# Forming twelve segments' value projections while a two-layer kernel's weights load, and reordering the loads

## The chip, the cores and the metric

The kernel runs on one core of one Trainium2 chip. A core has a tensor engine (PE, with weight loads shown apart as PEld), a vector engine (DVE), a scalar engine (ACT), GpSimd (POOL), and SyncE (SP), which here does nothing but issue DMAs. The metric is the device time of one execution in microseconds (us); the figure for a kernel is the median over its runs. The profile is that of a single execution.

## What is computed

Two kinds of layers alternate: A, B, A, B. Each adds to a residual stream x of 2048 tokens of width 512, after a layer norm. Layer A is a recurrent attention with a memory of 8 rows; layer B is a dense layer with a relu. Both A layers share their weights, and so do both B layers.

```python
# A: S = 2048, Dm = 512, H = 32 heads, Dh = 128, M = 8 memory rows, seg_len = 32
mem = mem0
for s in range(n_seg):                      # 64 segments, one after the other
    xs = x[:, s * seg_len:(s + 1) * seg_len, :]
    h = concat([mem, xs])                   # 40 rows
    q, k, v = h @ Wq, h @ Wk, h @ Wv        # 32 heads of 128
    p = softmax(where(mask, q @ k.T * scale, -1e9))
    o = (p @ v) @ Wo
    mem = o[:, :M, :]                       # handed to the next segment
    outs.append(o[:, M:, :])
# B: h = relu(x @ w1) @ w2, inner width 1376
x = x + A(layernorm(x)); x = x + B(layernorm(x))
x = x + A(layernorm(x)); x = x + B(layernorm(x))
```

The memory rows chain the segments of a layer one behind the other. The token rows of a segment do not depend on the chain: in the first layer their layer norm, and so their values `v`, can be formed at any time once x and Wv are there.

## The kernel before

**Tiling over time.** `step(k)` works on segment k of the first attention layer (index 0) and at once on segment k - 4 of the second (index 1), for k from 0 to 67 (`DELTA` is 4). `act` lists the layers that take part; in steps 0 to 3 it is only layer 0, in the last four only layer 1. Blocks of 64 tokens (two segments) pass through output projection, dense layer and residual in filler work that lies between the pieces of the steps; the dense layer first runs in step 3.

**A step.** HT holds the 40 transposed input rows of each layer: 8 memory columns (copied from the PSUM tile `mt` of the step before by DVE, L671) and 32 token columns (L535, or L391 and on for the second layer). Heads go in two halves of 16. For each half: `qk` forms Q and K (L404), then `scores` (L438), `exponents`, `probabilities`, `transpose_p` (L476) and `weighted_v` (L491, tile `pv`). Scores of the second half follow only after the first half's probabilities have been transposed. At the end `output_mem` (L445) multiplies the memory rows with Wo, ACT copies the result to `wm_sb` (L653), four matmuls turn it into `mt` (L668), and DVE and ACT copy that into the next step's HT and HTm (the memory rows alone).

**Values.** `weighted_v` reads the values from one tile Vs, rows 0 to 39 for layer 0 and 64 to 103 for layer 1, tokens in the rows from M = 8 on. `group_values` (L240) forms values for up to 32 rows at a time, four matmuls side by side in 32-column strips of the array, 512 output columns each; a segment takes two groups of 16. ACT copies each group to a tile VmS (L245, three buffers), and a DMA puts it into DRAM (L246); later `load` (L275) brings rows into Vs. The memory rows' values go that way in each step (tile `vmd`), the token rows' through `vd`.

In the first layer, segments 0 to 3 and all odd segments have their token values formed by `values0`: segment 0 in step 0, 1 and 2 in steps 0 and 1 between scores and the second half, and from segment 3 on segment k + 3 at the end of the even step k, after `mt`. Even segments from 4 on ride in free columns of the memory rows' group (`rider`, `first_rider`) and cost no matmuls.

**Order.** The main part lies in a block in which the program order is the order on PE, DVE, ACT and SP. POOL is not among them; its instructions are placed by the scheduler, as are the loads before the block. SP issues nearly all DMAs from one queue, in order; step 0 uses POOL's queue for its values. Tiles in PSUM: three buffers `c`, two `fill`, one for each layer's scores, one for the output projection.

**Loads.** The weights come in 1 MB pieces (8 heads of one matrix): Wq and Wk pieces 0 and 1, four of Wv, Wq and Wk pieces 2 and 3, four of Wo. The token rows come as pairs of 128 rows (`load_pair`), normalized and transposed by `pair_moments`, `pair_normalize` and `pair_T`. `load_dense` loads w1 and w2 in step 1.

Of the kernel before, what the change touches and what calls it, by code (L numbers as in the profile page):

```python
# [7 lines left out]
BF = mybir.dt.bfloat16  # L8
F32 = mybir.dt.float32
# [13 lines left out]
def kernel(  # L23
# [14 lines left out]
    nc = tc.nc  # L38
    _, S, Dm = A_x.shape
# [5 lines left out]
    L = M + SEG  # L45
# [33 lines left out]
    def load_pair(n):  # L79
        pairs["x", n] = wk.tile([128, Dm], BF, tag="xe", bufs=1, name="xe")  # L80
        nc.sync.dma_start(out=pairs["x", n][:], in_=A_x[0, 128 * n:128 * n + 128, :])
# [22 lines left out]
    Wo_v = A_Wo.rearrange("h e d -> e h d")  # L104
    PW = H * Dh // 4
    hh = H // 4

    def load_w(W_sb, W_v, pc):
        nc.sync.dma_start(out=W_sb[:, :, pc * PW:(pc + 1) * PW], in_=W_v[:, :, pc * PW:(pc + 1) * PW])  # L109

    for pc in range(2):
        load_w(Wq_sb, Wq_v, pc)
        load_w(Wk_sb, Wk_v, pc)
    for pc in range(4):
        load_w(Wv_sb, Wv_v, pc)
    for pc in range(2, 4):
        load_w(Wq_sb, Wq_v, pc)
        load_w(Wk_sb, Wk_v, pc)
    for pc in range(4):
# [4 lines left out]
    def load_dense():  # L124
        nc.sync.dma_start(out=w1_sb[:], in_=B_w1.rearrange("(c p) f -> p c f", p=128))
        nc.sync.dma_start(out=w2_sb[:, 0:NFC - 1, :],
                          in_=B_w2[0:(NFC - 1) * 128, :].rearrange("(c p) d -> p c d", p=128))
        nc.sync.dma_start(out=w2_sb[0:F_LAST, NFC - 1, :], in_=B_w2[(NFC - 1) * 128:Dff, :])
# [37 lines left out]
    nc.gpsimd.memset(P[:], 0.0)  # L166
    PT = const.tile([128, 8, 2, L], BF)
    OTx0 = const.tile([128, 2, H // 2, 128], BF)
    nc.vector.memset(OTx0[:], 0.0)
    OTx1 = const.tile([128, H // 2, 128], BF)  # L170
    nc.vector.memset(OTx1[:], 0.0)
    OTm = const.tile([128, H, 32], BF)
    nc.gpsimd.memset(OTm[:], 0.0)
    wm_sb = const.tile([128, Dm], BF)
    xn1 = const.tile([128, Dm], BF)
    nc.gpsimd.memset(xn1[:], 0.0)

# [23 lines left out]
        nc.vector.tensor_scalar(out=out[sl, :], in0=R[sl, :], scalar1=mv[sl, 0:1], scalar2=rstd[sl, 0:1],  # L201
                                op0=ALU.subtract, op1=ALU.mult)

    def transpose_x(xn, tag, bufs):
        tp = ps_fill.tile([128, NC4, 128], BF, tag="fill")
        for c4 in range(NC4):
            nc.tensor.transpose(tp[:, c4, :], xn[:, c4 * 128:(c4 + 1) * 128], ident[:])  # L207
        xnT = wk.tile([128, NC4, 128], BF, tag=tag, bufs=bufs, name=tag)
        nc.scalar.copy(out=xnT[:], in_=tp[:])
        return xnT  # L210


# [8 lines left out]
    def pair_T(n):  # L221
        pairs["T", n] = transpose_x(pairs["n", n], "xnT0", 2)

    def tokens_T(s, lo, n):

        c = SEG * (s % 4) + lo
        return pairs["T", s // 4][:, :, c:c + n]

# [2 lines left out]
    def group_values(lhsT, ii, dst, pool, tag, q, lo=0, hi=NC4):  # L233
        if lo == 0:
            vps[tag] = pool.tile([128, 512], F32, tag=tag, name="vp")
        vp = vps[tag]
        for c4 in range(lo, hi):
            for j in range(4):
                n = 4 * ii + j
                nc.tensor.matmul(vp[32 * j:32 * j + 32, :], lhsT=lhsT(c4), rhs=Wv_sb[:, c4, n * 512:(n + 1) * 512],  # L240
                                 start=(c4 == 0), stop=(c4 == NC4 - 1), tile_position=(0, 32 * j))
        if hi < NC4:
            return
        VmS = wk.tile([128, 512], BF, tag="VmS", bufs=3, name="VmS")
        nc.scalar.copy(out=VmS[:], in_=vp[:])  # L245
        q.dma_start(out=dst[ii].rearrange("j t e -> (j t) e"), in_=VmS[:])  # L246

    def dram_values(name, tag, bufs):
        return dram.tile([2, 4, 32, 512], BF, tag=tag, bufs=bufs, name=name)
# [5 lines left out]
    def values0(s, ii, q=None, lo=0, hi=NC4):  # L255

        if ii == 0 and lo == 0:
            vds[0, s] = dram_values("vd0", "vd0", 4)
        t = tokens_T(s, 0, SEG)
        group_values(lambda c4: t[:, c4, :], ii, vds[0, s], *((ps_fill, "fill") if ii else (ps_c, "c")), q or nc.sync, lo, hi)  # L260
# [14 lines left out]
        q.dma_start(out=Vs[lo:lo + n, 2048 * ii:2048 * (ii + 1)].rearrange("t (j e) -> t j e", j=4),  # L275
                    in_=vd[ii, :, t:t + n, :].rearrange("j t e -> t j e"))

    def load_tokens0(k, q):
        for ii in range(2):
            if first_rider(k):  # L280
                load(q, ii, M, 16, vmds[k - 2], 16)
                load(q, ii, M + 16, 16, vmds[k - 1], 16)
            else:
                load(q, ii, M, SEG, vds[0, k], 0)
# [173 lines left out]
            nc.scalar.activation(out=es[:], in_=es[:], func=ACTF.Exp, scale=SCALE)  # L458
        return ess

    def probabilities(hf, ess, a):

        es = ess[a]
        sm = wk.tile([128, 8], F32, tag="sm", bufs=2, name="sm")
        nc.vector.tensor_reduce(out=sm[:], in_=es[:], axis=AX.X, op=ALU.add)  # L465
        nc.vector.reciprocal(out=sm[:], in_=sm[:])
        eng = nc.vector if hf == 1 and a == max(ess) else nc.gpsimd
        eng.tensor_tensor(out=P[:, :, 64 * a:64 * a + L], in0=es[:],  # L468
                          in1=sm[:].unsqueeze(2).to_broadcast([128, 8, L]), op=ALU.mult)

# [40 lines left out]
    def step(k):  # L511
# [17 lines left out]
        with tc.high_priority(offset=PRIO):  # L529
            for a in act:  # L530
                if k == a * DELTA:
                    nc.vector.tensor_copy(out=HT[:, :, a, 0:M], in_=mem0T[:])
                    nc.vector.tensor_copy(out=HTm[:, :, a * M:(a + 1) * M], in_=mem0T[:])
            if 0 in act:
                nc.gpsimd.tensor_copy(out=HT[:, :, 0, M:L], in_=tokens_T(k, 0, SEG))  # L535
        if pr is not None:
            pair_moments(pr)

# [8 lines left out]
        qks = qk(HT, 0, act, after0)  # L547
        if dw is not None:
            dense_T(dw)
        if k == 0:  # L550
            for ii in range(2):
                values0(0, ii, nc.gpsimd)
        q = nc.gpsimd if k == 0 else nc.sync
        with tc.high_priority(offset=PRIO):
            if 0 in act:
                load_tokens0(k, q)
            vmds[k] = dram_values("vmd", "vmd", 4)
            for ii in range(2):
                group_values(lambda c4: HTm[:, c4, :], ii, vmds[k], ps_c, "c", q)
            if 1 in act and even:  # L560
                values1(k, 0)
            for ii in range(2):
                for a in act:
                    load(q, ii, 64 * a, M, vmds[k], a * M)
                if 1 in act and (ii == 0 or not even):
                    load(q, ii, 64 + M, SEG, vds[1, k], 0)
            scores(qks, act)
            if 1 in act and even:
                values1(k, 1)
                load(q, 1, 64 + M, SEG, vds[1, k], 0)  # L570
# [3 lines left out]
            ess = exponents(act)  # L574
        if dw is not None:
            dense_h(dw, 2, 3)
        if k < 2:
            for ii in range(2):
                values0(k + 1, ii)
        if k == 1:  # L580
            load_dense()
        if ldp is not None:
            load_pair(ldp)
        if not even and p + 1 < NP and p >= 1:
            load_x(p + 1)

        def after1(n):
            if n == 0:
                probabilities(0, ess, act[-1])
            if n == 1:  # L590
                masks(act, 1)

        if len(act) > 1:
            probabilities(0, ess, act[0])
        qks = qk(HT, 1, act, after1)

        def v0(ii):
            if even and k + 3 < NSEG:
                values0(k + 3, ii)

        def v1(ii):
            if even and k >= DELTA:
                values1(k + 1, ii)
# [10 lines left out]
            ess = exponents(act)  # L614


        v1(0)
        if dw is not None:
            dense_y(dw, 0, NFC)
# [6 lines left out]
            output_x(nw, 0, XA)  # L626
        with tc.high_priority(offset=PRIO):
            for a in act:
                probabilities(1, ess, a)
            if first:  # L630
                hand_on(dw)
            transpose_p()
            if first:
                block_moments(dw + 2)
        if dw is not None and dw >= 2:
            store(dw)
        if w is not None:
            output_x(w, XE, H)
        if nw is not None:
# [40 lines left out]
    with tc.manual_schedule(engines={mybir.EngineType.PE, mybir.EngineType.DVE, mybir.EngineType.SP,  # L680
                                    mybir.EngineType.Activation}):
        mem0T = const.tile([128, NC4, M], BF)
        tp = ps_fill.tile([128, NC4, 128], BF, tag="fill", name="tp0")
        for c4 in range(NC4):
            nc.tensor.transpose(tp[:, c4, :], mem0[:, c4 * 128:(c4 + 1) * 128], ident[:])
        nc.vector.tensor_copy(out=mem0T[:], in_=tp[:, :, 0:M])
        pair_moments(0)
        pair_normalize(0)
        pair_T(0)
        load_pair(1)  # L690
        for k in range(NSTEP):
            step(k)
        i = NT - 1
        output_x(i, XD, H)
        add_output(i)
        dense_moments(i)
        dense_normalize(i)
        dense_T(i)
        dense_h(i, 0, 3)
        dense_y(i, 0, NFC)  # L700
        store(i)
# [35 lines left out]
```

## Time and profile before

| what | us |
|---|---|
| median of 3 runs | 1709.79 (1708.37 to 1710.15) |
| the profiled execution | 1710.79 |
| its span, first to last instruction | 1709.0 |
| PE busy in the span | 1646.5 |
| mean granted clock of PE | 0.989 |

A row of the timeline has the start, the length, the engine, the line of the kernel, the operation, output tile and inputs, partitions by elements, a count where like instructions were merged, and in brackets how long the engine had been idle before it and what ended that. A row of the windows has a stretch of the span, the busy time of PE, of PE's weight loads, of DVE, ACT and POOL with their instruction counts, PE's granted clock, the busy share of the 16 DMA engines and the GB/s they moved. Matmuls are pipelined, so a busy PE isn't always a PE at its peak. A row by tile has the least, median and greatest duration in ns of one instruction, first and last start, and the shape.

### The profile page before, as it was taken

The numbers are of one execution on the slowest core, as the hardware profiler recorded it, in microseconds if no ns is written. First come the engines' busy times: TensorE is split into PE (matmuls) and PEld (weight loads), VectorE is DVE, ScalarE is ACT, GpSimd is POOL, SyncE is SP. The second block draws the span as 40 slices with busy tenths as digits, with TensorE's granted clock in tenths as the row PEclk, the third lists the DMA queues.
The fourth block names the chain that finished last, engine by engine and source line by source line (L and its number), as shares of the span: only waits on it lengthen the run. The fifth ranks groups of instructions, "written<-read, shape, count | busy, mean of one in ns | idle before, by whom it ended". The sixth has DMA issues, their size and how long they took to land.

```text
span 1709.0 us, 84178 instructions
## 1 busy us (share of the span) xinstructions
PE 1646.5 (96%) x37785; PEld 1202.4 (70%) x37876; DVE 1062.8 (62%) x2534; ACT 870.1 (51%) x2413; POOL 244.4 (14%) x457
## 2 busy tenths in 40 slices
PE   4799999999999999999999999999999999999997
PEld 2577777776777777677777767777776777777766
DVE  2356666666766666676666667666666766666644
ACT  1345555555555555555555555555555555555543
POOL 3011111111111111111111111111111111111100
PEclk9799999999999999999999999999999999999999
DMA  9612122121212212121221212122121212112111
GB/s 349 190 41 70 58 66 61 54 67 54 69 59 65 62 53 67 53 69 59 66 60 54 66 54 67 61 66 60 55 66 54 69 58 68 54 54 63 42 45 35
DMA packets 115513, 118.90 MB, mean 70 GB/s; under 512 B 14040, under 2 KB 106240, under 8 KB 115152
## 3 DMA queue, kind: packets, MB, share of 16 engines
q1 hardware_dynamic: 112240, 108.46, 20.4%
q8 instruction: 297, 4.87, 1.3%
q0 software_dynamic: 2912, 5.05, 1.1%
q14 instruction: 64, 0.52, 0.1%
HBM read 65.74 MB, written 45.61 MB: 65 GB/s over the span
## 4 chain that ended last, share of the span: by engine, by line
PE 93%; SPq 2%; DMA 2%; issue 1%; DVE 1%; ACT 0%; POOL 0%; POOLq 0%; DVEq 0%; ACTq 0%
PE qp L404 35%; PE vp L240 18%; PE wox L305 12%; PE sp L445 7%; PE hp L340 5%; PE pv L491 4%; PE yp L359 4%; PE sp L438 4%; PE tp L476 3%; SPq L109 2%; DMA Wo_sb<-in_A_Wo_dram 1%; SPq L120 1%; PE tp L207 1%; PE wox L289 1%; DMA vd<-VmS 1%
## 5 line engine op out<-in xcount | busy, mean ns | idle before, releaser
L404 PE MATMUL qp<-HT,Wq_sb 128*128 128x80 bf16 (+1 forms) x8704 | 370.0, 200 | 5.0 <-ACT VmS L245 3.1
L404 PE MATMUL qp<-HT,Wk_sb 128*128 128x80 bf16 (+1 forms) x8704 | 369.6, 200 | 2.8 <-DMA Wk_sb<-in_A_Wk_dram 2.8
L410 DVE CAST KT<-qp 128x480 bf16<-128x480 f32 (+3 forms) x340 | 202.8, 597 | 264.4 <-PE qp L404 259.0
L404 PEld LDWEIGHTS <-Wq_sb 128*128 128x128 bf16 x8704 | 330.1, 100 | 41.2 <-issue 33.7
L404 PEld LDWEIGHTS <-Wk_sb 128*128 128x128 bf16 x8704 | 328.7, 100 | 3.1 <-DMA Wk_sb<-in_A_Wk_dram 3.1
L408 ACT CAST QT<-qp 128x480 bf16<-128x480 f32 (+3 forms) x340 | 173.1, 509 | 254.3 <-PE qp L404 254.2
L245 ACT CAST VmS<-vp 128x512 bf16<-128x512 f32 x332 | 194.0, 585 | 162.3 <-PE vp L240 153.0
L305 PE MATMUL wox<-Wo_sb,OTx 128*128 128x512 bf16 x899 | 223.9, 379 | 9.9 <-issue 9.7
L468 POOL TENSOR_TENSOR P<-es,sm 128x320 bf16<-128x320 f32 x188 | 136.0, 723 | 580.2 <-ACT QT L408 155.9
L453 DVE TENSOR_REDUCE mx<-sp 128x8 f32<-128x320 f32 x256 | 114.5, 487 | 150.0 <-PE sp L438 149.6
L465 DVE TENSOR_REDUCE sm<-es 128x8 f32<-128x320 f32 x256 | 120.6, 471 | 73.2 <-ACT es L458 65.2
L305 PEld LDWEIGHTS <-OTx 128*128 128x128 bf16 x960 | 83.0, 98 | 104.5 <-issue 26.9
L240 PE MATMUL vp<-Wv_sb,HT 128*32 128x512 bf16 x2048 | 134.2, 382 | 0.0
L445 PE MATMUL sp<-Wo_sb,OTm 128*32 128x512 bf16 x2144 | 131.2, 387 | 1.4 <-DMA Wo_sb<-in_A_Wo_dram 1.4
L240 PE MATMUL vp<-Wv_sb,HTm 128*32 128x512 bf16 x2176 | 131.1, 382 | 0.0
L507 DVE CAST OTx<-pv 128x256 bf16<-128x256 f32 x256 | 91.2, 418 | 36.9 <-ACT OTm L499 35.9
L458 ACT ACTIVATE es<-es 128x320 f32<-128x320 f32 x256 | 109.3, 467 | 9.3 <-DVE es L456 2.8
L456 DVE TENSOR_TENSOR es<-sp,mx 128x320 f32<-128x320 f32 x256 | 113.4, 482 | 0.6
L477 ACT CAST PT<-tp 128x320 bf16<-128x320 f32 x136 | 58.3, 428 | 90.6 <-PE tp L476 90.6
L499 ACT CAST OTm<-pv 128x64 bf16<-128x64 f32 x512 | 80.4, 225 | 45.1 <-PE pv L491 45.0
L507 ACT CAST OTx<-pv 128x256 bf16<-128x256 f32 x256 | 84.8, 385 | 32.5 <-PE pv L491 32.5
L196 POOL TENSOR_TENSOR rstd<-rstd,mhalf_t 128x1 f32<-128x1 f32 (+1 forms) x82 | 45.3, 553 | 384.0 <-DVE rstd L195 384.0
(88 smaller groups left out, 1811.4 us busy)
## 6 DMA issues: line engine op xcount, KB each, us to landing
vd<-VmS SPq DMA_DIRECT2D x194, 128.0 KB
Vs<-vd SPq DMA_DIRECT2D x194, 128.0 KB
vmd<-VmS SPq DMA_DIRECT2D x134, 128.0 KB
Vs<-vmd SPq DMA_DIRECT2D x254, 32.0 KB
Vs<-vmd SPq DMA_DIRECT2D x120, 64.0 KB
Wq_sb<-in_A_Wq_dram SPq DMA_DIRECT2D x4, 1024.0 KB
Wk_sb<-in_A_Wk_dram SPq DMA_DIRECT2D x4, 1024.0 KB
R<-in_A_x_dram POOLq DMA_DIRECT2D x32, 128.0 KB, 2.9
```

What stands on the lines that cost most here:

```text
L240: nc.tensor.matmul(vp[32 * j:32 * j + 32, :], lhsT=lhsT(c4), rhs=Wv_sb[:, c4, n * 512:(n + 1) * 512], start=(c4 == 0), stop=(c4 == NC4 - 1 ...
L245: nc.scalar.copy(out=VmS[:], in_=vp[:])
L305: nc.tensor.matmul(wo_tiles[i][:], lhsT=ot, rhs=Wo_sb[:, h, :], start=(h == 0), stop=(h == H - 1))
L404: nc.tensor.matmul(qp[:, hi, 0:ncol], lhsT=W_sb[:, c4, h * Dh:(h + 1) * Dh], rhs=HT[:, c4, a_lo:a_hi, :], start=(c4 == 0), stop=(c4 == NC4 ...
L408: nc.scalar.copy(out=dst[:, 0:nh, a_lo * L:a_hi * L], in_=qp[:, 0:nh, 0:ncol])
L410: nc.vector.tensor_copy(out=dst[:, 0:nh, a_lo * L:a_hi * L], in_=qp[:, 0:nh, 0:ncol])
L445: nc.tensor.matmul(wo[32 * j:32 * j + 32, :], lhsT=OTm[:, h, :], rhs=Wo_sb[:, h, :], start=(h < 4), stop=(h >= H - 4), tile_position=(0, 3 ...
L453: nc.vector.tensor_reduce(out=mxs[a][:], in_=sp_tiles[a], axis=AX.X, op=ALU.max)
L456: nc.vector.tensor_tensor(out=es[:], in0=sp_tiles[a], in1=mxs[a][:].unsqueeze(2).to_broadcast([128, 8, L]), op=ALU.subtract)
L465: nc.vector.tensor_reduce(out=sm[:], in_=es[:], axis=AX.X, op=ALU.add)
L468: eng.tensor_tensor(out=P[:, :, 64 * a:64 * a + L], in0=es[:], in1=sm[:].unsqueeze(2).to_broadcast([128, 8, L]), op=ALU.mult)
L507: copy(out=ot[:, 8 * q:8 * q + 8, c:c + SEG], in_=pvs[q, a][:, :, M:L])
```

## The change

- Loads: Wv's four pieces come first, then Wq and Wk piece by piece in turn, then Wo. The rows of two sets of four odd segments (`SETS[1]`: 5, 7, 9, 11; `SETS[2]`: 13, 15, 17, 19) are loaded in between, by four DMAs a set, into tiles of 128 rows that serve other ends later.
- `set_values(j, lo, hi)` forms values of four segments at once: 128 token rows are the stationary operand, 512 columns of Wv stream, four matmuls make one chunk of 512 columns, eight chunks a set. Chunks are copied by DVE and ACT in turn (set 2: by ACT alone) into `stage(j, n)`, space in w1_sb and w2_sb, and for part of set 2 in OTx0, which are not yet in use. `set_store` then puts a set into DRAM, 1 MB.
- Before step 0: set 0 (segments 0 to 3), the memory rows' values of step 0 and their loads on POOL's queue, set 1, and two chunks of set 2. In step 0: four chunks of set 2 before the second half's probabilities and two before its `weighted_v`.
- `load_tokens0` takes segment 0 straight from `stage`, and the other eleven from the set in DRAM by one DMA of 32 rows. `values0` is gone for these twelve; the others stay as they are.
- SP: sets 0 and 1 are stored in step 0, set 2 in step 1 just ahead of `load_dense`, which now overwrites what the stores read. `load_pair` of step 1 goes ahead of `load_dense`.
- Smaller edits: OTx0 and OTx1 are no longer cleared; steps 0 and 1 copy tokens into HT on DVE, and step 0 multiplies P on DVE, each on POOL before.

```diff
+    SETS = ((0, 1, 2, 3), (5, 7, 9, 11), (13, 15, 17, 19))
+    set_of = {s: (j, n) for j, ss in enumerate(SETS) for n, s in enumerate(ss)}
+    def load_odd(j):
+        odd_x[j] = wk.tile([128, Dm], BF, tag="ob", bufs=1, name="xo") if j == 1 else wm_sb
+        for n, s in enumerate(SETS[j]):
+            nc.sync.dma_start(out=odd_x[j][SEG * n:SEG * n + SEG, :], in_=A_x[0, SEG * s:SEG * s + SEG, :])
...
-    for pc in range(2):
-        load_w(Wq_sb, Wq_v, pc)
-        load_w(Wk_sb, Wk_v, pc)
+    load_w(Wv_sb, Wv_v, 0)
+    load_w(Wv_sb, Wv_v, 1)
+    load_odd(1)
+    load_w(Wv_sb, Wv_v, 2)
+    load_w(Wv_sb, Wv_v, 3)
+    load_odd(2)
     for pc in range(4):
-        load_w(Wv_sb, Wv_v, pc)
-    for pc in range(2, 4):
         load_w(Wq_sb, Wq_v, pc)
         load_w(Wk_sb, Wk_v, pc)
...
+    def set_values(j, lo, hi):
+        xnT = odd_T[j] if j else pairs["T", 0]
+        for n in range(lo, hi):
+            vp = ps_fill.tile([128, 512], F32, tag="fill", name="vp")
+            for c4 in range(NC4):
+                nc.tensor.matmul(vp[:], lhsT=xnT[:, c4, :], rhs=Wv_sb[:, c4, n * 512:(n + 1) * 512],
+                                 start=(c4 == 0), stop=(c4 == NC4 - 1))
+            (nc.scalar.copy if n % 2 or j == 2 else nc.vector.tensor_copy)(out=stage(j, n), in_=vp[:])
+
+    def set_store(j, q):
+        set_dram[j] = dram.tile([128, H * Dh], BF, tag=f"set{j}", bufs=1, name="vset")
+        for lo, hi in ((0, 8),) if j < 2 else ((0, 2), (2, 5), (5, 8)):
...
+            q.dma_start(out=set_dram[j][:, 512 * lo:512 * hi], in_=src)
...
+        if k in set_of:
+            j, n = set_of[k]
+            q.dma_start(out=Vs[M:L, :], in_=set_dram[j][SEG * n:SEG * n + SEG, :])
+            return
...
-        eng = nc.vector if hf == 1 and a == max(ess) else nc.gpsimd
+        eng = nc.vector if k == 0 or hf == 1 and a == max(ess) else nc.gpsimd
...
-                nc.gpsimd.tensor_copy(out=HT[:, :, 0, M:L], in_=tokens_T(k, 0, SEG))
+                (nc.vector if k < 2 else nc.gpsimd).tensor_copy(out=HT[:, :, 0, M:L], in_=tokens_T(k, 0, SEG))
...
-        if k < 2:
-            for ii in range(2):
-                values0(k + 1, ii)
-        if k == 1:
-            load_dense()
         if ldp is not None:
             load_pair(ldp)
+        if k == 0:
+            set_store(0, nc.sync)
+            set_store(1, nc.sync)
+        if k == 1:
+            set_store(2, nc.sync)
+            load_dense()
...
-            if even and k + 3 < NSEG:
+            if even and k + 3 < NSEG and k + 3 not in set_of:
                 values0(k + 3, ii)
...
+        if k == 0:
+            set_values(2, 2, 6)
         v1(0)
...
+        if k == 0:
+            set_values(2, 6, 8)
         if w is not None:
             output_x(w, XE, H)
...
         pair_T(0)
+        odd_moments(1)
+        odd_normalize(1)
+        set_values(0, 0, 8)
+        nc.vector.tensor_copy(out=HTms[0][:, :, 0:M], in_=mem0T[:])
+        memory_values(0, nc.gpsimd)
+        load_tokens0(0)
+        for ii in range(2):
+            load(nc.gpsimd, ii, 0, M, vmds[0], 0)
+        odd_transpose(1)
+        odd_moments(2)
+        odd_normalize(2)
+        set_values(1, 0, 8)
+        odd_transpose(2)
         load_pair(1)
+        set_values(2, 0, 2)
```

## What I predict

> **What bounds the kernel now.** I read the engine totals first, then the span in a few long windows, then the timeline of the start, then the ends of single steps.
>
> ```profile
> PE 1646.5 (96%) x37785; PEld 1202.4 (70%) x37876; DVE 1062.8 (62%) x2534; ACT 870.1 (51%) x2413; POOL 244.4 (14%) x457
> ...
> 0.00:60.00 60.00, 30.20 (x506) 17.92 (x510) 14.52 (x39) 11.96 (x28) 14.61 (x38) 0.83 0.94 310
> 60.00:110.00 50.00, 46.51 (x1238) 34.67 (x1230) 22.96 (x60) 22.85 (x61) 3.96 (x10) 0.94 0.36 112
> 110.00:1609.00 1499.00, 1481.51 (x33922) 1084.59 (x34005) 976.66 (x2317) 795.27 (x2209) 219.67 (x399) 1.00 0.20 60
> ```
>
> After the totals, each row is a window: busy time of PE, PE's weight loads, DVE, ACT and POOL with counts, granted clock, DMA share, GB/s. From 110 us on PE is busy 1481.5 of 1499.0 us: PE work taken out there comes off the time, unless a wait appears in its place. In the first 60 us PE is busy for half and the DMA engines for 0.94: there the weights bound the kernel. So PE work that moves from the second stretch into idle time of the first is worth nearly all of itself.
>
> ```profile
> 20.87 0.61 PE L240 MATMUL vp<-Wv_sb,xnT 128*32 128x512 bf16 x2 [2.17 <-DMA Wv_sb<-in_A_Wv_dram]
> 23.58 1.89 PE L240 MATMUL vp<-Wv_sb,xnT 128*32 128x512 bf16 x14 [2.10 <-DMA Wv_sb<-in_A_Wv_dram]
> ...
> 41.63 0.71 PE L404 MATMUL qp<-HT,Wk_sb 128*128 128x40 bf16 x16 [0.46 <-DMA Wk_sb<-in_A_Wk_dram]
> ...
> 43.24 0.70 PE L476 MATMUL tp<-ident,P 128*128 128x80 bf16 x8
> ...
> 46.55 0.71 PE L491 MATMUL pv<-PT,Vs 40*128 40x40 bf16 x16 [2.21 <-DMA Vs<-vmd]
> ...
> 55.23 1.04 PE L445 MATMUL sp<-Wo_sb,OTm 128*32 128x512 bf16 x8 [1.44 <-DMA Wo_sb<-in_A_Wo_dram]
> ```
>
> The columns are start, length, engine, line, operation, tiles, count, and in brackets PE's wait before it and what ended it. A 1 MB weight piece lands every 2.71 us (20.87, 23.58). The last Wk piece lands at 41.6, the last Wo piece at 55.2. Step 0 waits for both, and once, 2.2 us, for its values.
>
> **What moves.** The values of segments 0 to 3 and odd 5 to 19, twelve in all, leave the steps. One segment is 32 matmuls, four side by side:
>
> ```profile
> L240 PE MATMUL vp<-Wv_sb,xnT x1088: 379/379/634, 20.9 to 1540.0; 128*32 128x512 bf16 x182
> ...
> 242.60 0.26 PE L668 MATMUL mt<-sel,wm_sb 128*128 128x16 bf16 x4
> 242.79 1.91 PE L240 MATMUL vp<-Wv_sb,xnT 128*32 128x512 bf16 x32
> 244.63 1.03 PE L404 MATMUL qp<-HT,Wq_sb 128*128 128x80 bf16 x24
> ...
> 1588.01 0.26 PE L668 MATMUL mt<-sel,wm_sb 128*128 128x16 bf16 x4
> 1588.59 1.02 PE L404 MATMUL qp<-HT,Wq_sb 128*128 128x80 bf16 x24 [0.32 <-DVE HT L671]
> ...
> 1635.91 0.26 PE L668 MATMUL mt<-sel,wm_sb 128*128 128x16 bf16 x4
> 1636.45 0.76 PE L404 MATMUL qp<-HT,Wq_sb 128*128 128x40 bf16 x24 [0.28 <-DVE HT L671]
> ```
>
> The 1088 matmuls are 34 segments; 22 stay. At the end of an even step the values stand between `mt` and the next step's projections and hide DVE's copy into HT. With that cover gone the copy is exposed, and the trace shows it, since the last even steps form no values: `mt` to the next projection takes 244.63 - 242.60 = 2.03 with them, 0.58 without, 0.54 where one layer runs. So steps 4 to 16 gain 7 x 1.45 and step 2 gains 1.49: **11.6 us**.
>
> ```profile
> 56.96 0.27 PE L668 MATMUL mt<-sel,wm_sb 128*128 128x16 bf16 x4 [0.69 <-ACT wm_sb L653]
> 57.16 3.60 PE L240 MATMUL vp<-Wv_sb,xnT 128*32 128x512 bf16 x32
> 60.70 0.98 PE L404 MATMUL qp<-HT,Wq_sb 128*128 128x40 bf16 x24
> 64.56 1.91 PE L240 MATMUL vp<-Wv_sb,HTm 128*32 128x512 bf16 x32
> 66.40 0.37 PE L438 MATMUL sp<-KT,QT 128*40 128x40 bf16 x16
> 71.95 0.46 PE L476 MATMUL tp<-ident,P 128*128 128x80 bf16 x8
> 82.03 0.78 PE L404 MATMUL qp<-HT,Wq_sb 128*128 128x40 bf16 x24
> 85.44 1.91 PE L240 MATMUL vp<-Wv_sb,HTm 128*32 128x512 bf16 x32
> 87.28 0.37 PE L438 MATMUL sp<-KT,QT 128*40 128x40 bf16 x16
> 91.35 0.46 PE L476 MATMUL tp<-ident,P 128*128 128x80 bf16 x8 [0.19 <-POOL P L468]
> ...
> 40.00:60.00 20.00, 12.76 (x208) 7.62 (x211) 5.76 (x15) 5.54 (x17) 3.06 (x6) 0.50 0.80 234
> ...
> 60.00:62.00 2.00, 2.00 (x47) 1.31 (x40) 0.00 (x0) 0.87 (x2) 0.00 (x0) 0.50 0.19 66
> 64.00:66.00 2.00, 2.00 (x54) 1.29 (x54) 1.00 (x3) 0.63 (x2) 0.00 (x0) 1.00 0.06 14
> ```
>
> Segment 3 at the end of step 0 ran at clock 0.50: 60.70 - 56.96 = 3.74, against 0.54 without, gains **3.2**. Segment 2 in step 1 lies between scores and transposes: 71.95 - 66.40 = 5.55, while step 2, which has none there, takes 4.07: **1.48**. Step 1's first projections took 3.86 at the low clock, step 2's 3.41; with PE at work in the start I expect full clock there: **0.45**. Segments 0 and 1 lay ahead of the last Wk piece and give nothing by themselves. Gains: 16.7 us.
>
> **What is added at the start, and its cover.** A set of four segments is 8 chunks of four 128x128 by 512 matmuls. The form is output_x's:
>
> ```profile
> 235.91 2.32 PE wox L305 x10
> ```
>
> 0.232 us each, so 0.93 a chunk and about 1.9 at clock 0.50. Before step 0's second half PE now has 18 chunks (16.7), the memory rows' values (1.84), two transposes with their copy (about 1.0), the first half's projections (3.41) and scores (0.37).
>
> ```profile
> 7.74 0.69 DVE L191 BATCH_NORM_STATS2 stats<-xe 128x6 f32<-128x512 bf16 x1
> 9.52 0.41 DVE L201 TENSOR_SCALAR xn<-xe,mv,rstd 128x512 bf16<-128x512 bf16 x1 [0.68 <-POOL rstd L196]
> ...
> 10.64 0.59 ACT L209 COPY xnT<-tp 128x512 bf16<-128x512 bf16 x1 [8.55 <-PE tp L207]
> ```
>
> PE can begin at 11.2, when the first tokens are transposed. But DVE has odd set 1's moments and normalization ahead of its first copy out of PSUM. Those rows come behind two Wv pieces, at 13 by my estimate (the third piece had landed before 14), and take 2.2 us (7.74 to 9.93). Two PSUM buffers let PE run two chunks and then stop; the third starts at about 15.9. From there 16 chunks, 1.84, 1.0, 3.41, 0.37 and some 2.8 for three chunks at the low clock end at 40. The second half, 3.4 us, then ends at about 43.6, and before it ended at 43.2. The twelve pieces ahead of Wo, and nearly the bytes beside them, are the same in another order (256 KB of token rows come, segment 0's 512 KB of trips go), so I leave 41.6 and 55.2 where they are. The cover is just full: cost 0, bounds -0.5 (nothing left to gain but the Wo wait) and +6.5 (below).
>
> Six chunks of set 2 lie in step 0's tail, four between weighted_v and the second transposes, two before the second weighted_v. There pv now finds its values early (2.2 us) and Wo's wait was 1.4. I walked it: transposes from 43.24, scores and pv end at 45.2; four chunks at the low clock (7.4) end at 52.6, while exponents and P on DVE and ACT pass under them; transposes 0.5, two full-clock chunks 1.9, pv 0.6, ACT's copies 0.5 that don't overlap, output_mem 1.9 end at 58.0, not at 56.3: **+1.7**. All six at full clock cost 0, all six at the low one +4.5 (both worked the same way). I take four, because the clock came up late last time: PE worked from 55.2 almost without a break, and the clock was 0.50 until past 62. [...]
>
> SP: eight loads of 32 KB go out ahead, some 0.4 us of issue each (as the dense row below), while the weights fill the queue. set_store 0 and 1 stand behind Wo and pair 1's load, so they delay neither. Step 1's token load waits for store 0 (landing about 59 by 2.7 us a MB), its pv comes at about 67. load_dense waits for set_store 2; behind it on SP stand step 2's loads.
>
> ```profile
> 70.35 0.44 SPq L125 DMA_DIRECT2D w_sb<-in_B_w_dram  x1
> ```
>
> It should again go out near 70: cost 0, and if late up to 3 us in step 2. The load of pair 2 now passes ahead of it, cost 0. The memsets of OTx0 and OTx1 go from DVE, which then waits for the same first loads. Steps 0 and 1 copy tokens on DVE instead of POOL, step 0 multiplies P there: a few tenths, off the path.
>
> **Sum.** 16.7 - 1.7 = 15.0 off the profiled execution's 1710.79 gives 1695.8. The median of the runs is 1.0 lower: **1694.8**.
>
> **Rivals.**
> *The tail stays cold.* PE waits before the second half, the clock is 0.50 through all six chunks and step 1's start: 4.5 + 0.45, so 16.7 - 4.95 = 11.75 and 1698.0. For it: 0.50 from 40 to 62 in the trace. Against: PE now has work where it idled.
>
> *POOL blocks set 2's normalization.* POOL's order isn't written by hand:
>
> ```profile
> 26.39 0.58 POOL L246 DMA_DIRECT2D vd<-VmS  x1 [14.57 <-ACT VmS L245]
> 31.82 0.59 POOL L275 DMA_DIRECT2D Vs<-vd  x1 [4.86 <-DMA vd<-VmS]
> 32.40 0.56 POOL L246 DMA_DIRECT2D vd<-VmS  x1
> ...
> vmd<-VmS POOLq DMA_DIRECT2D x2, 128.0 KB, 6.2
> ```
>
> There a store stood behind a load that waited 4.86 us. If the power of odd set 2 stands behind the loads of the memory rows (stores, 6.2 to land, two issues), DVE's normalization and with it set 1's copies wait, about 8.5 us, of which 2 have slack: 6.5 lost, 1699.6. Against: its inputs are ready before those loads can be.
>
> *The values were cover for a slower trip.* The memory rows go through DRAM between values and pv; if that trip bound the steps, the 11.6 would not come: 1706.4. Against: the trip starts after the first projections and moves with pv, and the last even steps show only 0.3.
>
> *Slower.* Both POOL's wait and the low clock, with the first 18 chunks not fitting: from 15.9 six chunks 11.1, memory rows 3.6, stores, landing and loads 8.5, power and normalization 1.0, six chunks and a copy 11.7, transposes 1.0, two chunks 3.7, both halves 9: 65.5 in place of 43.2. With 4.5 in the tail the delay is 27 against 16.7: 1720. It decides from 17 us of delay. Against: continuous work raised the clock in the trace each time.
>
> **How the numbers follow.** Forecast 0.52 (own range 1689 to 1698.0), cold tail 0.20, POOL 0.10, cover 0.07, slower 0.11. The range from 1688 (tail free, the Wo wait of 1.4 gone, a few us of low clock less) to 1705 leaves out the slower and the cover case, 0.18, and a little below. No change, within 0.2% or 3.4 us, is about what this kernel's measurement can't tell: 0.03 from partly slower starts; faster 0.86, slower 0.11.
>
> **What would show it.** L240 with xnT at 704 matmuls, a new line with 96; `mt` to projection near 0.58 in steps 4 to 16; second-half transposes of step 0 near 43.5 and `mt` near 58.7. A first projection of step 1 past 61, POOL's power behind a waiting load, or PE waits on Vs in steps 1 and 2 would make it wrong.

## The result, and the profile after

| | before | after |
|---|---|---|
| median, us | 1709.08 (4 runs, 1707.08 to 1710.15) | 1694.13 (4 runs, 1691.85 to 1694.54) |
| ratio, 95% interval | | 0.9911 (0.9894 to 0.9928) |
| profiled execution | 1710.79 | 1691.85 |
| its span | 1709.0 | 1690.2 |

The change saves 15.0 us. 1694.8 was forecast. The two profiled executions lie 18.9 apart, because that of before is slower than its four runs and that of after the fastest of its own; a second profile of the changed kernel, below, tells which of its gains belong to the one execution.

The totals of the page after, and the same long windows (totals first, then window, length, busy time of PE, PE's weight loads, DVE, ACT, POOL with counts, granted clock, DMA share, GB/s):

```profile
PE 1652.1 (98%) x37596; PEld 1199.2 (71%) x37596; DVE 1068.5 (63%) x2551; ACT 865.2 (51%) x2407; POOL 242.0 (14%) x453
```

```profile
0.00:60.00 60.00, 43.32 (x598) 24.66 (x599) 21.24 (x58) 19.45 (x42) 12.79 (x34) 0.94 1.02 341
60.00:110.00 50.00, 44.46 (x1248) 35.39 (x1245) 28.08 (x73) 22.71 (x65) 5.30 (x13) 1.00 0.38 122
```

PE does as much as before (1652 against 1646 us), but 43.3 us of it in the first 60, where it was 30.2. PE's tiles by the view of `vp`:

```profile
L286 PE MATMUL vp<-Wv_sb,xnT x704: 378/379/391, 474.8 to 1523.4; 128*32 128x512 bf16 x176
...
L264 PE MATMUL vp<-Wv_sb,xnT x32: 377/380/635, 11.2 to 19.9; 128*128 128x512 bf16 x32
L264 PE MATMUL vp<-Wv_sb,dnT x32: 377/379/390, 23.4 to 31.1; 128*128 128x512 bf16 x32
L264 PE MATMUL vp<-Wv_sb,hT x32: 378/380/635, 32.6 to 53.5; 128*128 128x512 bf16 x32
```

The 704 and three times 32 matmuls are those forecast: twelve segments are gone from L286, and the three sets stand at 11 to 20, 23 to 32 and 33 to 54 us. The timeline of PE at the start, and at steps 1, 2 and 4 (`issue` in the brackets is time for which the profile shows nothing that the engine waited for):

```profile
11.20 9.10 PE L264 MATMUL vp<-Wv_sb,xnT 128*128 128x512 bf16 x32 [0.68 <-ACT xnT L220]
...
38.36 0.78 PE L464 MATMUL qp<-HT,Wq_sb 128*128 128x40 bf16 x24
...
44.13 0.72 PE L464 MATMUL qp<-HT,Wk_sb 128*128 128x40 bf16 x16 [2.10 <-DMA Wk_sb<-in_A_Wk_dram]
45.74 0.70 PE L536 MATMUL tp<-ident,P 128*128 128x80 bf16 x8
47.41 4.46 PE L264 MATMUL vp<-Wv_sb,hT 128*128 128x512 bf16 x16
56.05 0.61 PE L505 MATMUL sp<-Wo_sb,OTm 128*32 128x512 bf16 x8 [0.26 <-DMA Wo_sb<-in_A_Wo_dram]
57.36 0.26 PE L730 MATMUL mt<-sel,wm_sb 128*128 128x16 bf16 x4 [0.69 <-ACT wm_sb L715]
58.00 0.77 PE L464 MATMUL qp<-HT,Wq_sb 128*128 128x40 bf16 x24 [0.39 <-DVE HT L596]
61.30 1.91 PE L286 MATMUL vp<-Wv_sb,HTm 128*32 128x512 bf16 x32
63.14 0.38 PE L498 MATMUL sp<-KT,QT 128*40 128x40 bf16 x16
66.84 0.46 PE L536 MATMUL tp<-ident,P 128*128 128x80 bf16 x8
72.10 1.91 PE L505 MATMUL sp<-Wo_sb,OTm 128*32 128x512 bf16 x32
81.74 0.40 PE L286 MATMUL vp<-Wv_sb,HTm 128*32 128x512 bf16 x3 [1.00 <-issue]
86.92 0.56 PE L551 MATMUL pv<-PT,Vs 40*128 40x40 bf16 x16 [0.36 <-DMA Vs<-vmd]
...
136.64 0.26 PE L730 MATMUL mt<-sel,wm_sb 128*128 128x16 bf16 x4
137.21 1.02 PE L464 MATMUL qp<-HT,Wq_sb 128*128 128x80 bf16 x24 [0.32 <-DVE HT L733]
```

PE is through with its early work at 38.4 and meets late weights again: the last Wk piece at 44.1, the last Wo piece at 56.1. From `mt` to the next projection step 4 takes 0.57. The starts of `mt` at the ends of steps are the clock by which all runs below are compared:

| `mt` of step | 0 | 1 | 2 | 3 | 5 | 9 | 13 | 17 | 60 | 64 |
|---|---|---|---|---|---|---|---|---|---|---|
| before | 56.96 | 81.30 | 99.24 | 120.13 | 168.70 | 268.49 | 368.31 | 467.93 | 1538.25 | 1635.91 |
| after | 57.36 | 74.73 | 93.68 | 113.07 | 160.28 | 256.94 | 353.61 | 450.57 | 1521.71 | 1617.29 |
| gained | -0.4 | 6.6 | 5.6 | 7.1 | 8.4 | 11.6 | 14.7 | 17.4 | 16.5 | 18.6 |

The gain is made by step 17, 1.5 us at a time after step 3. Of the 18.6 at step 64, 2.6 came between steps 63 and 64, where the changed code is the same as the old one: the profile of before took 23.4 us there and that of after 20.8, and the run of the old code with the weights in another order took 21.2. Most of that difference belongs to the profile of before alone.

### The profile page after: what moved, and what is told of

Its sections match the earlier page's. It is cut to its first block, busy times and chain, and to the rows that moved or that the text cites. A ratio compares the mean times of both kernels' runs of the same rounds, so it can differ in the third digit from the quotient of the medians.

```text
span 1690.2 us, 83651 instructions
## 1 busy us (share of the span) xinstructions
PE 1652.1 (98%) x37596; PEld 1199.2 (71%) x37596; DVE 1068.5 (63%) x2551; ACT 865.2 (51%) x2407; POOL 242.0 (14%) x453
## 3 DMA queue, kind: packets, MB, share of 16 engines
q8 instruction: 295, 4.83, 1.2%
## 4 chain that ended last, share of the span: by engine, by line
PE 93%; DMA 3%; SPq 2%; DVE 1%; ACT 1%; issue 0%; POOL 0%; POOLq 0%; DVEq 0%; ACTq 0%
PE qp L464 35%; PE vp L286 16%; PE wox L365 13%; PE sp L505 7%; PE hp L400 5%; PE yp L419 4%; PE pv L551 4%; PE sp L498 4%; PE tp L536 3%; DMA Wv_sb<-in_A_Wv_dram 1%; SPq L134 1%; PE tp L218 1%; SPq L122 1%; DMA Wo_sb<-in_A_Wo_dram 1%; DMA vmd<-VmS 1%; PE wox L349 1%
## 5 line engine op out<-in xcount | busy, mean ns | idle before, releaser
L291 ACT CAST VmS<-vp 128x512 bf16<-128x512 f32 x308 | 179.7, 583 | 140.8 <-PE vp L286 133.5
L365 PE MATMUL wox<-Wo_sb,OTx 128*128 128x512 bf16 x960 | 237.4, 380 | 0.0
L286 PE MATMUL vp<-Wv_sb,HT 128*32 128x512 bf16 x2048 | 133.4, 381 | 0.0
L286 PE MATMUL vp<-Wv_sb,HTm 128*32 128x512 bf16 x2176 | 130.3, 381 | 1.0 <-issue 1.0
```

The source lines that it names most:

```text
L365: nc.tensor.matmul(wo_tiles[i][:], lhsT=ot, rhs=Wo_sb[:, h, :], start=(h == 0), stop=(h == H - 1))
```

## The experiments

**The moved work put back.** The value matmuls of one segment and their two copies stand again at the end of the even steps 2 to 16; their result is neither stored nor read.

```diff
-        q.dma_start(out=dst[ii].rearrange("j t e -> (j t) e"), in_=VmS[:])
+        if dst is not None:
+            q.dma_start(out=dst[ii].rearrange("j t e -> (j t) e"), in_=VmS[:])
...
             if even and k + 3 < NSEG and k + 3 not in set_of:
                 values0(k + 3, ii)
+            elif even and k >= 2 and k + 3 in set_of:
+                t = tokens_T(k + 3, 0, SEG)
+                group_values(lambda c4: t[:, c4, :], ii, None, *((ps_fill, "fill") if ii else (ps_c, "c")), None)
```

> The changed kernel, with the 32 value matmuls of one segment and their two ACT copies put back at the end of steps 2 to 16, as work whose result nobody reads; no DMA comes with them, and the twelve segments still take their values from the sets. Theory (PE work moved out of a PE-bound stretch): 8 x 1.45 = 11.6 us come back, 1694.1 + 11.6 = about 1705.7, and mt to the next projection is 2.03 again in steps 4 to 16. Rival (the gain came from the DRAM trips that went, or from ACT's copies): well below, 1694 to 1698. Either way step 1 begins near 58.

Measured: 1706.41 us, 0.9983 (0.9973 to 0.9993) of the kernel before. PE's timeline at the end of step 4, and in step 2:

```profile
86.40 0.52 PE L286 MATMUL vp<-Wv_sb,HTm 128*32 128x512 bf16 x3 [2.53 <-issue]
...
143.75 0.26 PE L734 MATMUL mt<-sel,wm_sb 128*128 128x16 bf16 x4
143.94 1.91 PE L286 MATMUL vp<-Wv_sb,xnT 128*32 128x512 bf16 x32
145.78 1.03 PE L465 MATMUL qp<-HT,Wq_sb 128*128 128x80 bf16 x24
```

2.03 from `mt` to the projection, as before. Against the kernel before, `mt` is 0.2 us early at step 3 and 0.4 late at step 17: the loop gains nothing any more. No DMA came back with the work, so the trips through DRAM were worth nothing here. ACT's two copies did come back, and the run alone doesn't part them from PE's work; the rows do: PE forms values for 1.91 of the 2.03 us and goes on without a wait. Step 2 lost 2.5 us in a place that the experiments on the dense loads explain.

**Set 0 alone.** Sets 1 and 2 are undone, with their loads, chunks and stores.

```diff
-    SETS = ((0, 1, 2, 3), (5, 7, 9, 11), (13, 15, 17, 19))
+    SETS = ((0, 1, 2, 3),)
...
-    load_odd(1)
...
-    load_odd(2)
...
-            set_store(1, nc.sync)
...
-            set_store(2, nc.sync)
...
-        if k == 0:
-            set_values(2, 2, 6)
...
```

> Only segments 0 to 3 are formed while the weights load; sets 1 and 2, with their row loads, chunks and stores, are undone, and the eight odd segments go back to the even steps. Theory: the eight segments cost 11.6 again and the start gains next to nothing, since mt of step 0 is bound by Wo: 1705 to 1706. Rival (the sets crowd the start, and 2.5 us of it were lost because the last Wk piece landed at 44.1 rather than 41.6): 1702 to 1703.5. If the odd rows' loads are what delays the last Wk piece, it lands near 41.6 here; if it is POOL's traffic for step 0's values, it stays near 44.

Measured: 1704.14 us, 0.9968 (0.9953 to 0.9984), between the theory's 1705 and the rival's 1703.5. The timeline of its step 0:

```profile
42.51 0.72 PE L462 MATMUL qp<-HT,Wk_sb 128*128 128x40 bf16 x16 [1.75 <-DMA Wk_sb<-in_A_Wk_dram]
...
54.34 1.04 PE L503 MATMUL sp<-Wo_sb,OTm 128*32 128x512 bf16 x8 [1.66 <-DMA Wo_sb<-in_A_Wo_dram]
56.08 0.27 PE L722 MATMUL mt<-sel,wm_sb 128*128 128x16 bf16 x4 [0.69 <-ACT wm_sb L707]
```

`mt` of step 0 comes at 56.08, 1.3 earlier than with three sets; at step 17 the gain is 5.7 and not 17.4. The difference, 11.6, is the figure forecast for the even steps, and from step 2's `mt` to step 17's they do make 11.5 of it. Up to there three other things nearly cancel: the two sets cost 1.3 us in step 0 and 1.4 in step 2 (an idle time explained below), and step 1 is 2.8 shorter with them (17.37 from `mt` to `mt` against 20.16), since set 0 alone begins it at half clock (0.50 from 52 to 57 us, 0.55 from 57 to 62). In the change's second profile step 1 takes 18.77, and the difference at step 17 is 9.55; by the medians the two sets are worth 10.0. In step 0 the last Wo piece lands 1.7 later with them, the last Wk piece 1.6 later. The 0.9 us by which Wk is late here as well (41.6 before) is not the odd rows'.

**The order of the weights alone**, in the kernel before.

```diff
-    for pc in range(2):
-        load_w(Wq_sb, Wq_v, pc)
-        load_w(Wk_sb, Wk_v, pc)
     for pc in range(4):
         load_w(Wv_sb, Wv_v, pc)
-    for pc in range(2, 4):
+    for pc in range(4):
         load_w(Wq_sb, Wq_v, pc)
         load_w(Wk_sb, Wk_v, pc)
```

> The kernel before, with only the order of the weights changed: Wv's four pieces first, then Wq and Wk in turn, then Wo. Theory: no gain by itself, since step 0 still waits for the last Wk and the last Wo piece; segment 0's trip through DRAM starts later than before, so 0 to 4 us slower, 1709 to 1713. Rival (the order is what gains): 1700 or below. The last Wk piece should land at 41.6 if the order alone doesn't move it.

Measured: 1710.73 us, 1.0006 (0.9997 to 1.0015). From its timeline:

```profile
48.97 0.71 PE L488 MATMUL pv<-PT,Vs 40*128 40x40 bf16 x16 [4.69 <-DMA Vs<-vmd]
...
58.27 0.28 PE L665 MATMUL mt<-sel,wm_sb 128*128 128x16 bf16 x4 [0.69 <-ACT wm_sb L650]
```

Step 0's values, formed after the first projections, now reach Vs 2.4 us later (48.97 against 46.55), and `mt` is 1.3 late. By itself the order gains nothing; it only lets the values be formed early.

**All of set 2 ahead of step 0.**

```diff
-        if k == 0:
-            set_values(2, 2, 6)
...
-        if k == 0:
-            set_values(2, 6, 8)
...
-        set_values(2, 0, 2)
+        set_values(2, 0, 8)
```

> The changed kernel, with all eight chunks of set 2 ahead of step 0 and none in its tail. Theory: PE waits 3.4 us for the last Wq and Wk pieces there, so six chunks (5.2 us) delay the second half by about 1.8; the tail is 5.2 shorter, and mt of step 0 stays at 57.4, bound by the last Wo piece: 1693.5 to 1695. Rival (the chunks in the tail are on the path): mt 1 us or more earlier, 1692 to 1693. If the delay of the second half is more than the tail's saving, mt comes later than 57.4.

Measured: 1696.96 us, 0.9925 (0.9910 to 0.9939), 2.8 slower than the change (no run of it is as fast as any of the change's); I had expected no difference. Its start:

```profile
33.05 7.08 PE L264 MATMUL vp<-Wv_sb,hT 128*128 128x512 bf16 x31 [0.86 <-ACT hT L220]
...
48.05 0.56 PE L464 MATMUL qp<-HT,Wq_sb 128*128 128x40 bf16 x12 [2.38 <-issue]
...
50.31 0.70 PE L536 MATMUL tp<-ident,P 128*128 128x80 bf16 x8
54.37 0.71 PE L536 MATMUL tp<-ident,P 128*128 128x80 bf16 x8 [2.33 <-DVE P L528]
56.11 3.61 PE L505 MATMUL sp<-Wo_sb,OTm 128*32 128x512 bf16 x32
60.40 0.26 PE L726 MATMUL mt<-sel,wm_sb 128*128 128x16 bf16 x4 [0.69 <-ACT wm_sb L711]
```

The second half's transposes come at 50.3, not at the 47.5 that I had: PE stood 2.4 us in the middle of the projections without a cause that the trace shows. Then the tail has nothing to fill the 2.3 us for which PE waits on P, and at the low clock (0.50 from 52 to 57 us, 0.66 from 57 to 62) `output_mem` takes 3.6 us where it took 1.9. So the six chunks in the tail stand in part where PE would wait anyway. `mt` is 3.0 late, and 2.4 of that is the idle time without a cause. What remains, 0.7, is an estimate of what the place of the chunks is worth: the second half's transposes are 2.2 later without the idle time, and from there to the end of `output_mem` it takes 9.4 where it took 10.9. The run doesn't part the two any further.

**The dense weights' loads in step 2**, behind its own value loads, and **in pieces**, two of w1's four in step 1 and the rest with w2 in step 2.

```diff
             set_store(2, nc.sync)
-            load_dense()
+        if k == 2:
+            load_dense()
```

```diff
-        nc.sync.dma_start(out=w1_sb[:], in_=B_w1.rearrange("(c p) f -> p c f", p=128))
+        load_w1(2, 4)
+        load_w2()
+
+    def load_w1(lo, hi):
+        for c in range(lo, hi):
+            nc.sync.dma_start(out=w1_sb[:, c, :], in_=B_w1[128 * c:128 * c + 128, :])
+
+    def load_w2():
...
-            load_dense()
+            load_w1(0, 2)
+        if k == 2:
+            load_dense()
```

> The changed kernel, with the dense weights' three loads issued in step 2, behind that step's own value loads, instead of in step 1. In three profiles (the changed kernel, the one with the work put back, the one with the tail free) PE stood idle 1.0, 2.5 and 2.0 us with nothing to wait for at the same place, three or four matmuls before the end of step 2's memory-row values, while the dense weights were loading at some 370 GB/s. Theory (PE's instruction stream is fetched late beside the dense loads): the idle time at that place and the 0.4 us wait for Vs go, step 2 takes 17.5 to 17.9 instead of 18.95 from mt to mt, and the time is 1692 to 1693.5, unless a later place meets the loads. Rival (a stall of that instruction, whatever the loads do): it stays, 1694.

> The changed kernel, with w1 loaded in four pieces of 352 KB, two in step 1 at the old place and two in step 2 with w2. Theory as for the run with the loads in step 2: less is in flight at once, so the idle time in step 2's memory-row values goes, 1692 to 1693.5. Rival: it stays, 1694.

Measured: 1691.90 us, 0.9898 (0.9883 to 0.9913), and 1692.42, 0.9899 (0.9885 to 0.9914). The split's memory-row values in step 2, and the longest idle time without a cause of the run with the later loads, which lies in step 3:

```profile
80.87 1.91 PE L293 MATMUL vp<-Wv_sb,HTm 128*32 128x512 bf16 x32
```

```profile
97.73 0.42 PE L464 MATMUL qp<-HT,Wq_sb 128*128 128x40 bf16 x10 [0.56 <-issue]
```

Step 2 takes 17.56 and 17.57 us from `mt` to `mt`, against 18.95 in the change: the idle time goes and with it the 0.4 us wait for Vs. The later loads leave a smaller one in step 3, the split none from step 1 on.

**Step 1's token rows behind the dense weights.**

```diff
-        if ldp is not None:
+        if ldp is not None and k != 1:
             load_pair(ldp)
...
             load_dense()
+            load_pair(ldp)
```

> The changed kernel, with step 1's load of token rows (pair 2) put behind the dense weights again. Theory: those rows then land with the last of the dense weights, near 83, while DVE reaches their moments at about 76, in order ahead of the copies of K; PE runs out of PSUM buffers and waits: step 2 is 3 to 6 us longer, 1697 to 1700. Rival (the order of this load doesn't matter, as in the kernel before, where DVE waited 1.6 us for it off the path): 1694, and no wait of PE.

Measured: 1697.98 us, 0.9928 (0.9914 to 0.9943), 3.9 more than the change. In step 2:

```profile
82.58 0.69 DVE L202 BATCH_NORM_STATS2 stats<-xe 128x6 f32<-128x512 bf16 x1 [5.55 <-DMA xe<-in_A_x_dram]
...
84.05 3.04 PE L286 MATMUL vp<-Wv_sb,HTm 128*32 128x512 bf16 x32 [2.79 <-DVE KT L470]
```

DVE waits 5.55 us for the rows, K's copies stand behind that wait in its order, and PE, out of PSUM buffers, idles 2.8 and then starts at the low clock (0.78 from 82 to 87 us; 3.04 for 1.91). Step 2 takes 22.3. In the kernel before DVE waited 1.6 us for the same rows off the path; with step 2 coming some 5 us earlier that load became the bound.

**Steps 0 and 1 on POOL again.**

```diff
-        eng = nc.vector if k == 0 or hf == 1 and a == max(ess) else nc.gpsimd
+        eng = nc.vector if hf == 1 and a == max(ess) else nc.gpsimd
...
-                (nc.vector if k < 2 else nc.gpsimd).tensor_copy(out=HT[:, :, 0, M:L], in_=tokens_T(k, 0, SEG))
+                nc.gpsimd.tensor_copy(out=HT[:, :, 0, M:L], in_=tokens_T(k, 0, SEG))
```

> The changed kernel, with the token copies of steps 0 and 1 and step 0's product for P on POOL again. Theory (a few tenths, off the path): 1694 to 1694.7, step 0's mt within 0.5 of 57.4. Rival (POOL stands in a wait for step 0's value loads, and the copy into HT behind it): step 0's first projection starts later, as does its P, up to 3 us more.

Measured: 1692.78 us, 0.9907 (0.9890 to 0.9923): the same as the change within the runs' spread.

```profile
57.16 0.26 PE L730 MATMUL mt<-sel,wm_sb 128*128 128x16 bf16 x4 [0.69 <-ACT wm_sb L715]
57.70 0.76 PE L464 MATMUL qp<-HT,Wq_sb 128*128 128x40 bf16 x24 [0.28 <-DVE HT L733]
...
81.88 0.40 PE L286 MATMUL vp<-Wv_sb,HTm 128*32 128x512 bf16 x3 [1.45 <-issue]
```

`mt` of step 0 moves by 0.2, and the wait after it is 0.1 shorter, since the token copy isn't on DVE ahead of the projection. That edit of the change brings nothing.

**The change and the split once more, side by side.**

> The changed kernel itself, unchanged, beside the one with the dense weights split, on one chip. Theory: 1692 to 1695, and in its profile PE is again idle without a cause shown, 1 us or more, in step 2's memory-row values. If step 1's output_mem runs at half or mixed clock this time (2.4 us or more, not 1.9), the full clock there in the first profile was chance.

> The changed kernel with the dense weights split, as run once before. Theory: 1.0 to 1.5 us below the changed kernel in the same call, with no idle time in step 2's memory-row values. If it is within 0.5 us of it, the split is no gain that can be told.

Measured: 1693.48 us (1691.75 to 1694.73), 0.9912 (0.9898 to 0.9926), and 1691.82 (1690.53 to 1692.37), 0.9899 (0.9885 to 0.9913). The changed kernel's second profile:

```profile
73.13 2.53 PE L505 MATMUL sp<-Wo_sb,OTm 128*32 128x512 bf16 x32
...
83.57 0.40 PE L286 MATMUL vp<-Wv_sb,HTm 128*32 128x512 bf16 x3 [1.18 <-issue]
```

The idle time in step 2 is there again. Step 1's `output_mem` takes 2.53 and not 1.91, so the full clock in the first profile was chance; here the gain is 5.06 at step 3 and 15.3 at step 17. The chance can be seen. In the profile of before the clock stood at 0.50 from 39.10 to 62.99, 76.64 to 80.06, 1626.29 to 1629.71 and 1697.97 to 1704.80, in the change's first profile from 42.30 to 49.13: 23.89, 3.41, 3.41, 6.83 and 6.83 us, each 3.41 or a multiple of it, and within one profile the falls and rises lie multiples of 3.41 apart. That the clock changes only at the ends of intervals of that length, which lie elsewhere in each execution, is my reading of these traces; no run varies it. The 3.41 us ahead of the fall in the second profile, and in the first, counted on from the rise at 49.13, the interval with the least PE work within step 1:

```profile
67.60:71.01 3.41, 1.66 (x45) 1.27 (x44) 2.51 (x6) 1.75 (x6) 0.00 (x0) 1.00 0.65 229
```

```profile
69.60:73.01 3.41, 2.36 (x52) 1.64 (x56) 2.10 (x6) 0.85 (x4) 0.00 (x0) 1.00 0.68 268
```

Behind the 3.41 us with 1.66 of PE work the clock fell to half for as long (71.0 to 74.4, over `output_mem`); behind those with 2.36 it stayed at 1.00. From 67.40 to 70.81, which is no interval of that count, the first profile has as little PE work, 1.67 us, and the clock stayed as well. The split's median was 1.7 us below the change's both times (the first time with the two measured apart), by ratios whose intervals overlap: probably a little faster, and not shown beyond that.

## Why the prediction was right

**The even steps (11.6).** Right. The gains of steps 3, 5 and so on to 17 add up to 12.0 in the first profile. With the work put back they vanish; in the change's second profile they add up to 12.0 again. The price of the lost cover, read off the last even steps of the kernel before (0.58), is what steps 4 to 16 pay (0.57).

**Segment 3 and step 1 (3.2, 1.48, 0.45).** Right within 0.4. `mt` to the projection takes 0.64 where it took 3.74: 3.10. Scores to transposes 3.70 where it took 5.55: 1.85. The first projections 3.30 where they took 3.86: 0.56. What I hadn't in the sum is step 1's `output_mem`, 1.3 shorter in the first profile, 0.7 in the second.

**The start (cost 0).** Wrong by 2.5 us. "I leave 41.6 and 55.2 where they are" fell: the last Wk piece landed at 44.1 and the last Wo piece at 56.1, so the second half's transposes came at 45.7 and not near 43.5. The bytes beside the weights were as many as before: of segment 0's 512 KB only half went, since 256 KB still go from `stage` into Vs by a DMA. But at a DMA share of over one, two stretches of the start moved less than in the kernel before (its two rows first, then those of set 0 alone, then those of after):

```profile
8.00:20.00 12.00, 5.33 (x133) 4.88 (x132) 2.89 (x10) 1.60 (x4) 1.75 (x5) 1.00 1.09 352
24.00:28.00 4.00, 2.08 (x16) 0.42 (x9) 0.00 (x0) 0.59 (x1) 0.58 (x1) 1.00 1.05 387
```

```profile
8.00:20.00 12.00, 9.54 (x32) 3.80 (x33) 3.05 (x7) 2.34 (x4) 1.20 (x3) 1.00 1.09 351
24.00:28.00 4.00, 1.41 (x49) 1.20 (x45) 0.41 (x1) 0.57 (x2) 0.54 (x1) 0.92 1.05 328
```

```profile
8.00:20.00 12.00, 9.40 (x36) 3.82 (x36) 5.06 (x12) 2.34 (x4) 1.76 (x4) 1.00 1.12 330
24.00:28.00 4.00, 3.33 (x16) 1.38 (x15) 1.70 (x3) 0.70 (x2) 0.27 (x1) 1.00 1.05 327
```

1.6 of Wk's 2.5 us go with sets 1 and 2, whose one addition to the DMAs by then is the odd rows' 256 KB. They are loaded between 8 and 20 us, where the change alone is slower: 21 GB/s less over 12 us are 0.25 MB, the rows themselves 0.26, and both together take 1.4 us at the 370 GB/s that the kernel before moved from 12 to 20 us. The other 0.9 remain with set 0 alone, which has the dip from 24 to 28 us as well; the run with the order alone has no dip there (386 GB/s) and doesn't wait for Wk there. Which transfers are the slow ones was not tried. On PE's side I was too dear: no wait at the third chunk (the first odd rows had landed by 11.6, not 13), and the second half could begin at 38.4, not 40. So it was the weights, not the chunks, that bound the second half.

**The tail (+1.7).** Right in sign, too dear. `mt` came 0.4 late in the first profile and 0.65 in the second. From the second half's transposes to the end of `output_mem` the walk had 14.8 us, and it took 10.9 (45.74 to 56.66): the four chunks took 4.46 and not 7.4, because the clock was up again by 50 us.

```profile
38.89:42.30 3.41, 1.85 (x66) 1.64 (x62) 2.05 (x6) 1.10 (x4) 0.00 (x0) 1.00 1.05 383
42.30:45.71 3.41, 1.58 (x47) 1.58 (x48) 0.70 (x2) 0.31 (x1) 0.00 (x0) 0.50 1.10 352
45.71:49.13 3.42, 3.42 (x52) 2.11 (x49) 2.10 (x6) 1.67 (x5) 0.29 (x1) 0.50 1.09 350
50.00:55.00 5.00, 5.00 (x57) 2.56 (x59) 0.84 (x3) 3.78 (x10) 0.00 (x0) 1.00 1.10 362
```

So the tail began 2.5 late, since Wk was late, and was 3.8 shorter than the walk; `mt` came at 57.4, 1.3 ahead of the 58.7 that I had. That these two errors go against each other is luck. The rows are cut where the clock changed: it rose at about 49.1, 5 us after PE took up work at 44.1, and in the trace of before I had read 7 us (it rose at 62.99, 7.8 after 55.2). The clock also fell, at 42.3, behind 3.41 us in which PE was busy for 1.85 and waited 1.3 at the longest. So neither 5 nor 7 us is a fixed time.

**Step 2.** The prediction had SP's order cost it nothing, or up to 3 us by late loads. 1.4 were lost (18.95 against 17.56 without): 1.0 by PE standing idle beside the dense loads, which I hadn't thought of, and 0.4 by the wait for Vs, which the prediction had named as a sign of being wrong.

In sum, at step 3 I had 4.9 gained; the profiles say 7.1 and 5.1. From there to step 17 I had 10.15; they say 10.3 and 10.2. So the loop's share was right by its mechanism. That the median fell within 0.7 of the forecast owes something to luck in the first three steps: a start too cheap against a tail too dear, and step 1's `output_mem` against the idle time of step 2, neither of which the sum had. Of the rivals, the cold tail came true only up to 49.1, the cover case fell with the work put back, POOL's order did not block set 2 (its power ran at 23.7, ahead of the load that waited, at 29.0), and the slower case had no ground, as PE was early for the second half. POOL's 1699.6 was added up without the tail's 1.7; with it, it would have been 1701.3.

## What to carry to other kernels

Work that didn't depend on the chain and sat in a stretch that one engine bounds was worth its full length when it moved into that engine's idle time at the start, less the wait that it was covering (here 2.03 us from `mt` to the projection at the end of an even step, less 0.58); the end of the same kernel, where the work had run out, showed that wait's size before anything was changed. When a step begins earlier, look at every load that it needs: one that was off the path by a few microseconds can be on it then, as the token rows behind the dense weights were (DVE waited 1.6 us for them off the path, then 5.55 on it). A start that is bound by loads can pay for an added transfer by more than its bytes: here 256 KB in eight loads cost 1.6 us, about twice the time of their bytes at 370 GB/s (0.7). Filler in a tail that waits can be cheaper than the same work ahead of it; here that is an estimate of 0.7 us.

## What was not expected of the hardware

PE stood idle 1.0 to 2.5 us with nothing to wait for that the profile shows, in five profiles of the variants that load the dense weights in one go in step 1, and at the same place of the program: three or four matmuls before the end of step 2's memory-row values. In one variant it did so a second time, 2.4 us under the weights' load. The two variants that move or split the dense loads are free of it there, and so is set 0 alone, whose dense loads went out at 66.4 us, ahead of that place, and not at 72.0. With the token rows behind the loads PE came to the place only after its wait for K. That the stall goes with the loads is shown; in the profile after the DMA engines moved 371 GB/s from 78 to 80 us and 327 from 80 to 82, where PE stood. That PE's instructions came late is my reading of the traces; no run varies it. The page of the profile after has a row for a queue of instructions among the DMA queues:

```profile
q8 instruction: 295, 4.83, 1.2%
```

Its packets hold 16 KB each (4.83 MB in 295), and they make one for every 255 of PE's 75,192 matmuls and weight loads. The DMA view, asked for short windows, shows when each starts. The eighth packet starts 4.6, 4.7, 4.7, 5.1 and 5.6 us after step 1's `mt` in the five profiles with the stall (the change twice, POOL again, the tail free, the work put back), and PE goes on 2.5 to 3.0 us after the packet's start. In the three profiles with the dense loads later or split, whose program on PE is the change's, the same packet starts 1.7 to 2.0 us after that `mt`, and PE doesn't stand. The latest packets go with the longest stalls: 1.0 to 1.5 us at 4.6 and 4.7, 2.0 at 5.1, 2.5 at 5.6. The second idle time with the tail free has the same form: a packet starts at 45.4, and PE goes on at 48.05. What held the packet back beside the loads is not shown.
